# Loads cast by the DMA on one queue, and q and k in 72-partition runs, in a fused sliding-window attention and FFN kernel

## The chip, the cores and the metric

The kernel runs on one NeuronCore of a Trainium2 chip. The metric is device time in microseconds (us) of one execution, median over runs. The engines are TensorE (PE; its weight loads are PEld), VectorE (DVE), ScalarE (ACT), GpSimd (POOL) and SyncE (SP), which here only issues DMAs. 16 DMA engines serve all queues.

## The reference

Attention over q, k, v of shape (8 batches, 8 heads, 576 positions, 64), then an FFN over the 4608 tokens. Heads 0 to 3 see a window of the last 32 positions ("plain"), heads 4 to 7 every fourth of the last 128 ("dilated").

```python
rel = pos[:, None] - pos[None, :]
mask_plain = (rel >= 0) & (rel < 32)
mask_dil = (rel >= 0) & (rel < 128) & (rel % 4 == 0)
attn = softmax(where(mask, q @ k.T / 8, -1e9))      # per batch and head, f32
x = (attn @ v).transpose(0, 2, 1, 3).reshape(4608, 512)
h = relu(x @ w_in)                                  # w_in 512 x 2048
out = (h * h) @ w_out                               # w_out 2048 x 512
```

## The kernel before

**Attention** works on one batch and on pairs of heads: pair e (0 to 3) is heads 2e and 2e+1, pairs 0 and 1 plain, 2 and 3 dilated. `qT` holds q transposed, with the two heads' 64 dimensions one above the other on the partitions (rows 0 to 63 and 64 to 127) and positions along the free side; for dilated pairs the positions are sorted by residue modulo 4, so that a dilated window becomes a band again. `kbd` and `vbd` (two of the latter, for batches in turn) hold k and v as nine blocks of 64 positions, block-diagonal over the two heads: one head's block in rows and columns 0 to 63, the other's in 64 to 127, zeros elsewhere, written once by memsets. So one matmul over 128 rows serves both heads.

For each pair: `t_main` transposes q, then k, on PE against an identity into a PSUM tile `pa`, and copies evacuate it to `qT` and `kbd` (plain pairs on ACT, L209 and L223; dilated pairs on DVE, L204 and L218). `scores` (two halves) does the banded matmuls into `pa`, an Exp on ACT (L261) and a mask multiply on DVE (L262). `pv` (two halves) does P times V into `po` and, against a matrix `ones`, the row sums into `pd` (L304), then the reciprocal as Ln and Exp on ACT (L306, L307) and the product on DVE into `xT` (L310, L317), which the FFN reads. PSUM has four buffers for the FFN (`pf`), two for `pa`, one for `po` and one for `pd`.

**Loads.** SP's queue brings q, k and v as f32 into `raw` tiles, one set for all batches. Of q and k the first 512 positions are loaded with four consecutive positions on a partition (1 KB runs, L112) and the last 64 apart (`load_rem`, L120, 256 B runs); v by L131, L135 and L139. POOL then casts everything to bf16: `cast_qk` (L157, L163) into `rb` tiles, `cast_v` (L173) into the blocks of `vbd`. `t_rem` transposes the last 64 positions of all four pairs together and evacuates them with four DVE copies (L183, L186, L192). The FFN weights come on POOL's queue, cast by the DMA (L375, L380).

**FFN** takes 512 tokens at a time (9 tiles). A tile has 32 groups of four matmuls 128x512: 16 of `g1` (L343, then ReLU on ACT, L347, and a square on DVE, L348) and 16 of `g2` (L354; every fourth ends with a copy on ACT, L360, and a store by SP, L361).

**The order is written out by hand** (manual schedule; each engine executes in program order). Batch 0 is loaded, cast and its whole attention done before the first FFN group. Then, in the loop over tiles t, the loads of batch t+2 are issued first, and the attention of batch t+1 is woven between the groups: `attention_steps` gives each step the number of the group after which it is put (pair e begins at 1 + 7e: q, then k one later, scores at +3 and +4, pv at +6 and +8). The casts of batch t+2 are put on POOL four groups before the tile's end; POOL has nothing else, and starts each as soon as its data and its target are free.

Of the kernel before, what the change touches and what calls it, by code (L numbers as in the profile page):

```python
# [16 lines left out]
def _masks() -> np.ndarray:  # L17

    j = np.arange(64)[:, None]
    c = np.arange(96)[None, :]
    band = ((c - j >= 0) & (c - j < WIN)).astype(np.float32)
    kr, km = j % RES, j // RES
    cc = np.arange(64)[None, :]
    qr, qm = cc // 16, cc % 16
    rem = ((kr == qr) & (qm - km >= 0)).astype(np.float32)
    one = np.concatenate([band, rem], axis=1)
    return np.concatenate([one, one], axis=0).astype(ml_dtypes.bfloat16)  # L30
# [3 lines left out]
def kernel(  # L34
# [23 lines left out]
    MAIN = 512  # L58
# [8 lines left out]
    raw_pool = ctx.enter_context(tc.tile_pool(name="raw", bufs=1))  # L67
# [15 lines left out]
    ident = const.tile([P, P], bf16, name="ident")  # L83
    ones = const.tile([P, P], bf16, name="ones")
    mk = const.tile([P, 160], bf16, name="mk")
# [12 lines left out]
    raws = {}  # L98

    def load_qk(b: int, es):  # L100
        if b not in raws:
            raws[b] = {
                "q": raw_pool.tile([P, H, RES * D], f32, name="qraw"),
                "k": raw_pool.tile([P, H, RES * D], f32, name="kraw"),
                "qr": raw_pool.tile([64, H, D], f32, name="qrem"),
                "kr": raw_pool.tile([64, H, D], f32, name="krem"),
                "v": raw_pool.tile([P, NE, NB, D], f32, name="vraw"),
            }
        r = raws[b]
        hs = slice(2 * es[0], 2 * es[-1] + 2)  # L110
        for nm, src in (("q", q), ("k", k)):
            nc.sync.dma_start(  # L112
                r[nm][:, hs, :],
                src[b, hs, 0:MAIN, :].rearrange("h (p j) d -> p h (j d)", j=RES),
            )

    def load_rem(b: int):
        r = raws[b]
        for nm, src in (("qr", q), ("kr", k)):
            nc.sync.dma_start(  # L120
                r[nm][:, :, :], src[b, :, MAIN:S, :].rearrange("h p d -> p h d")
            )

    def load_v(b: int):
        r = raws[b]["v"]
        for hl in range(2):
            rows = slice(64 * hl, 64 * hl + 64)
            for e in range(NE):
                h = 2 * e + hl
                if e < NE // 2:  # L130
                    nc.sync.dma_start(  # L131
                        r[rows, e, :, :], v[b, h].rearrange("(i p) d -> p i d", p=64)
                    )
                else:
                    nc.sync.dma_start(  # L135
                        r[rows, e, 0:8, :].rearrange("p (m r) d -> p m (r d)", r=RES),
                        v[b, h, 0:MAIN, :].rearrange("(m p r) d -> p m (r d)", p=64, r=RES),
                    )
            nc.sync.dma_start(  # L139
                r[rows, NE // 2 : NE, 8, :],  # L140
                v[b, H // 2 + hl : H : 2, MAIN:S, :].rearrange("h p d -> p h d"),
            )


    rbs = {}

    def cast_qk(b: int, eng=None):
        eng = eng or nc.gpsimd
        r = raws[b]
        rbs[b] = {  # L150
            "q": rb_pool.tile([P, NE, RES, P], bf16, name="qb"),
            "k": rb_pool.tile([P, NE, RES, P], bf16, name="kb"),
            "qr": rb_pool.tile([64, NE, P], bf16, name="qrb"),
            "kr": rb_pool.tile([64, NE, P], bf16, name="krb"),
        }
        for nm in ("qr", "kr"):
            eng.tensor_copy(  # L157
                rbs[b][nm][:, :, :].rearrange("p e c -> p (e c)"),
                r[nm][:, :, :].rearrange("p h d -> p (h d)"),
            )  # L160
        for e in range(NE):
            for nm in ("q", "k"):
                eng.tensor_copy(  # L163
                    rbs[b][nm][:, e, :, :].rearrange("p j (h d) -> p h j d", h=2),
                    r[nm][:, 2 * e : 2 * e + 2, :].rearrange("p h (j d) -> p h j d", j=RES),
                )

    def cast_v(b: int):
        r = raws[b]["v"]
        for e in range(NE):  # L170
            for hl in range(2):
                rows = slice(64 * hl, 64 * hl + 64)
                nc.gpsimd.tensor_copy(vbd[b % 2][rows, e, :, 64 * hl : 64 * hl + 64], r[rows, e, :, :])  # L173


    def t_rem(b: int):
        ps = ps_a.tile([P, 1024], bf16, name="pa")
        for n, nm in enumerate(("qr", "kr")):
            for e in range(NE):
                c0 = 256 * n + 64 * e  # L180
                nc.tensor.transpose(ps[:, c0 : c0 + 64], rbs[b][nm][:, e, :], ident[0:64, 0:64])
        half = NE // 2
        nc.vector.tensor_copy(  # L183
            qT[:, 0:half, MAIN:S], ps[:, 0:128].rearrange("p (e c) -> p e c", c=64)
        )
        nc.vector.tensor_copy(  # L186
            qT[:, half:NE, :].rearrange("p e (r m) -> p e r m", r=RES)[:, :, :, 128:M],
            ps[:, 128:256].rearrange("p (e m r) -> p e r m", e=half, r=RES),
        )
        for hl in range(2):  # L190
            rows = slice(64 * hl, 64 * hl + 64)
            nc.vector.tensor_copy(  # L192
                kbd[rows, :, 8, 64 * hl : 64 * hl + 64],
                ps[rows, 256:512].rearrange("p (e c) -> p e c", c=64),
            )

    def t_main(b: int, e: int, nm: str):
        ps = ps_a.tile([P, 1024], bf16, name="pa")
        for j in range(RES):
            nc.tensor.transpose(ps[:, P * j : P * j + P], rbs[b][nm][:, e, j, :], ident[:, :])  # L200
        dil = e >= NE // 2
        if nm == "q":
            if dil:
                nc.vector.tensor_copy(  # L204
                    qT[:, e, :].rearrange("p (r m) -> p r m", r=RES)[:, :, 0:128],
                    ps[:, 0:MAIN].rearrange("p (r m) -> p r m", r=RES),
                )
            else:
                nc.scalar.copy(  # L209
                    qT[:, e, 0:MAIN].rearrange("p (m r) -> p m r", r=RES),  # L210
                    ps[:, 0:MAIN].rearrange("p (r m) -> p m r", r=RES),
                )
            return
        for hl in range(2):
            rows = slice(64 * hl, 64 * hl + 64)
            cols = slice(64 * hl, 64 * hl + 64)
            if dil:
                nc.vector.tensor_copy(  # L218
                    kbd[rows, e, 0:8, cols].rearrange("p (m r) c -> p r m c", r=RES),
# [183 lines left out]
    for _, step in attention_steps(0):  # L403
        step()
# [51 lines left out]
```

## Time and profile before

| What | us |
|---|---|
| median of 3 runs (399.03 to 404.46) | 400.42 |
| the profiled execution | 401.11 |
| its span in the profile | 399.3 |
| PE busy (modelled ends) | 321.9 |
| ACT, DVE, POOL busy | 208.5, 179.8, 98.3 |
| first FFN matmul begins | 62.1 |
| chain that ended last: PE 57%, ACT 13%, issue 10%, DVE 9% | |

The span is what the profile shows between the first and the last instruction; 1.8 us of the profiled execution lie outside it. Times within the trace count from the span's start. A group row gives line, engine, operation, target and source tile, shapes, count, then busy us and mean ns of one, then the idle time ahead of it and what ended it. "x4" in a timeline row means four merged instructions.

### The profile page before, as it was taken

To read this page: it belongs to the slowest core of one execution; us is meant where nothing else is said; L and a number is where in the kernel's file an instruction comes from. 1 tells how busy PE (TensorE), PEld (TensorE's weight loads), DVE (VectorE), ACT (ScalarE), POOL (GpSimd) and SP (SyncE) were. 2 spreads that over 40 slices of the span, in tenths; PEclk is the share of its full clock that TensorE was granted. 3 is DMA by queue.
4 is the path that set the end of the run, shared out by engine and by line. 5 is a ranking of instruction groups with operands and counts; after the bars stand their busy time and mean duration, and the time that the engine had idled before them with its cause. 6 is when DMAs were issued, how large, how long until landed. Compare 5 with 4: busy or idle time off the path is not lost.

```text
span 399.3 us, 5896 instructions
## 1 busy us (share of the span) xinstructions
PE 321.9 (81%) x2199; PEld 169.1 (42%) x2240; DVE 179.8 (45%) x365; ACT 208.5 (52%) x421; POOL 98.3 (25%) x158
## 2 busy tenths in 40 slices
PE   0201447999979997899699986999699999999996
PEld 0101333555535553455345543555345555444442
DVE  7100346653475347635763468336833543420410
ACT  1201434954873487448734792469346954742631
POOL 6423578300073007400640046003700000000000
PEclk9999999999998999999969998999899999999999
DMA  8999998001790179018901690149111001001002
GB/s 189 228 209 242 238 262 123 3 26 54 240 144 26 54 239 144 29 53 249 134 0 54 209 198 2 54 157 236 17 54 54 0 29 53 28 10 70 28 26 80
DMA packets 60557, 42.37 MB, mean 106 GB/s; under 512 B 31344, under 2 KB 55920, under 8 KB 60528
## 3 DMA queue, kind: packets, MB, share of 16 engines
q1 hardware_dynamic: 56160, 37.76, 39.0%
q0 software_dynamic: 4224, 4.19, 6.2%
q8 instruction: 17, 0.28, 0.3%
q10 hardware_dynamic: 144, 0.04, 0.1%
q14 instruction: 12, 0.10, 0.1%
HBM read 36.74 MB, written 9.44 MB: 116 GB/s over the span
## 4 chain that ended last, share of the span: by engine, by line
PE 57%; ACT 13%; issue 10%; DVE 9%; SPq 5%; DMA 5%; POOL 0%; ACTq 0%; POOLq 0%
PE pf L354 25%; PE pf L343 22%; ACT rec L307 4%; ACT rec L306 4%; DMA vraw<-in_v_dram 4%; DVE kbd L218 3%; DVE h2T L348 3%; PE po L304 3%; PE pd L304 2%; ACT kbd L223 2%; SPq L131 2%; ACT h2T L347 2%; PE pa L200 2%; DVE pt L262 2%; SPq L135 1%
## 5 line engine op out<-in xcount | busy, mean ns | idle before, releaser
L343 PE MATMUL pf<-xT,w_in_sb 128*128 128x512 bf16 x559 | 139.4, 386 | 1.2 <-issue 0.2
L354 PE MATMUL pf<-w_out_sb,h2T 128*128 128x512 bf16 x552 | 137.1, 386 | 1.3
L348 DVE TENSOR_TENSOR h2T<-h2T 128x512 bf16<-128x512 bf16 x144 | 92.8, 651 | 68.5 <-ACT h2T L347 67.0
L347 ACT ACTIVATE h2T<-pf 128x512 bf16<-128x512 f32 x144 | 84.6, 597 | 23.8 <-PE pf L343 23.3
L343 PEld LDWEIGHTS <-w_in_sb 128*128 128x128 bf16 x576 | 52.6, 99 | 51.7 <-issue 1.9
L354 PEld LDWEIGHTS <-h2T 128*128 128x128 bf16 x576 | 52.6, 99 | 51.1 <-issue 2.2
L306 ACT ACTIVATE rec<-pd 128x320 f32<-128x320 f32 (+1 forms) x64 | 26.3, 410 | 77.7 <-PE pd L304 77.7
L304 PE MATMUL po<-pt,vbd 128*128 128x96 bf16 (+3 forms) x320 | 24.2, 211 | 43.3 <-DVE pt L262 19.5
L173 POOL CAST vbd<-vraw 64x576 bf16<-64x576 f32 x64 | 46.4, 725 | 14.6 <-DMA vraw<-in_v_dram 11.3
L261 ACT ACTIVATE pt<-pa 128x480 bf16<-128x480 f32 (+1 forms) x64 | 32.3, 512 | 32.3 <-PE pa L246 27.4
L304 PEld LDWEIGHTS <-vbd 128*128 128x128 bf16 x320 | 22.1, 105 | 59.9 <-issue 30.1
L157 POOL CAST qrb<-qrem 64x512 bf16<-64x512 f32 x8 | 4.9, 606 | 164.3 <-PE pf L343 58.2
L310 DVE TENSOR_TENSOR xT<-po,rec 128x288 bf16<-128x288 f32 x32 | 14.7, 458 | 56.7 <-ACT rec L307 56.7
L360 ACT COPY osb<-pf 128x512 f32<-128x512 f32 x36 | 21.1, 587 | 35.7 <-PE pf L354 34.7
L317 DVE TENSOR_TENSOR xT<-po,rec 128x320 bf16<-128x320 f32 (+1 forms) x32 | 14.6, 456 | 37.3 <-ACT rec L307 33.9
L307 ACT ACTIVATE rec<-rec 128x320 f32<-128x320 f32 (+1 forms) x64 | 28.3, 443 | 2.0
L262 DVE TENSOR_TENSOR pt<-pt,mask_d 128x416 bf16<-128x416 bf16 (+1 forms) x32 | 12.8, 402 | 27.0 <-ACT pt L261 27.0
L304 PE MATMUL pd<-pt,ones 128*128 128x160 bf16 (+5 forms) x160 | 23.7, 250 | 0.0
L163 POOL CAST kb<-kraw 128x512 bf16<-128x512 f32 x32 | 19.4, 607 | 3.7 <-DMA kraw<-in_k_dram 3.7
L163 POOL CAST qb<-qraw 128x512 bf16<-128x512 f32 x32 | 19.4, 607 | 1.4 <-DMA qraw<-in_q_dram 1.4
L262 DVE TENSOR_TENSOR pt<-pt,mask_p 128x480 bf16<-128x480 bf16 (+1 forms) x32 | 16.9, 531 | 5.4 <-ACT pt L261 5.1
L223 ACT COPY kbd<-pa 64x512 bf16<-64x512 bf16 x32 | 18.3, 573 | 1.5 <-PE pa L200 1.3
(44 smaller groups left out, 183.0 us busy)
## 6 DMA issues: line engine op xcount, KB each, us to landing
out_dram<-osb SPq DMA_DIRECT2D x36, 256.0 KB, 2.0
qraw<-in_q_dram SPq DMA_DIRECT2D x7, 1024.0 KB, 5.7
kraw<-in_k_dram SPq DMA_DIRECT2D x7, 1024.0 KB, 8.5
vraw<-in_v_dram SPq DMA_DIRECT2D x32, 144.0 KB, 5.9
vraw<-in_v_dram SPq DMA_DIRECT2D x32, 128.0 KB, 5.4
w_in_sb<-in_moe_w_in_dram POOLq DMA_DIRECT2D x4, 512.0 KB, 13.1
w_out_sb<-in_moe_w_out_dram POOLq DMA_DIRECT2D x4, 512.0 KB, 25.2
qraw<-in_q_dram SPq DMA_DIRECT2D x2, 512.0 KB, 9.8
```

Source lines behind the costliest of these rows:

```text
L163: eng.tensor_copy(rbs[b][nm][:, e, :, :].rearrange("p j (h d) -> p h j d", h=2), r[nm][:, 2 * e : 2 * e + 2, :].rearrange("p h (j d) -> p ...
L173: nc.gpsimd.tensor_copy(vbd[b % 2][rows, e, :, 64 * hl : 64 * hl + 64], r[rows, e, :, :])
L223: nc.scalar.copy(kbd[rows, e, 0:8, cols].rearrange("p i (m r) -> p i m r", r=RES), ps[rows, 0:MAIN].rearrange("p (r i m) -> p i m r", r=RE ...
L261: nc.scalar.activation(pt[:, off : off + n], ps[:, 0:n], ACT.Exp, scale=SCALE)
L262: nc.vector.tensor_tensor(out=pt[:, off : off + n], in0=pt[:, off : off + n], in1=mask, op=ALU.mult)
L304: nc.tensor.matmul(oo, lh, rh, start=(x == 0), stop=(x == len(g) - 1), skip_group_check=True)
L306: nc.scalar.activation(rec[:, 0:n], d[:, 0:n], ACT.Ln)
L307: nc.scalar.activation(rec[:, 0:n], rec[:, 0:n], ACT.Exp, scale=-1.0)
L343: nc.tensor.matmul(ps1[:, :], w_in_sb[:, kt, P * f : P * f + P], xT[:, kt, tk0 : tk0 + NT], start=(kt == 0), stop=(kt == KT - 1),)
L347: nc.scalar.activation(h2[:, f, :], ps1[:, :], ACT.Relu)
L348: nc.vector.tensor_tensor(out=h2[:, f, :], in0=h2[:, f, :], in1=h2[:, f, :], op=ALU.mult)
L354: nc.tensor.matmul(cur[m][:, :], h2[:, f, P * m : P * m + P], w_out_sb[:, f, :], start=(f == 0), stop=(f == NF - 1),)
```

## The change

- q, k and v are loaded by POOL's queue, which casts them to bf16 on the way: q and k into `rb` tiles, v straight into the blocks of `vbd`. The `raw` tiles, `load_rem`, `cast_qk`, `cast_v` and `t_rem` are gone.
- q and k of a head lie on 72 partitions with 8 consecutive positions each (plain: 2 KB runs), or, for dilated heads, as two halves of 4 positions each (1 KB runs).
- `t_main` transposes per head, four transposes of a 72x128 block (two positions of 64 dimensions) into 72 columns each. The result has even positions (of the pair in the block) on rows 0 to 63 and odd ones on rows 64 to 127, so each evacuation copy takes one head and one half of the rows and moves it to that head's rows: dilated q is a DVE copy of 288 elements, dilated k DVE copies of 256 and 32, plain q and k an ACT copy of 288 each.
- The identity and the ones matrix come with the masks from DRAM; the memsets are put in another order.
- The loads of batch 0 are issued pair by pair in the order 0, 2, 1, 3, then the weights (w_in in two parts, not four), then batch 1. The last 64 positions of v of both dilated pairs come with the last pair's load.
- The attention of batch 0 (`first_attention`) is pipelined over the pairs and uses the `pf` buffers for its transposes. In FFN tile 0 the steps of batch 1 begin at group 12 with 5 groups a pair; later tiles begin at 0 with 7 a pair. The pairs go in the order 0, 2, 1, 3.

The diff, cut to its core:

```diff
     def load_qk(b: int, es):
...
+                if es_[0] < NE // 2:
+                    nc.gpsimd.dma_start(
+                        rbs[b][nm][:, hs, :], src[b, hs, :, :].rearrange("h (p j) d -> p h (j d)", j=JT)
+                    )
+                else:
+                    nc.gpsimd.dma_start(
+                        rbs[b][nm][:, hs, :].rearrange("p h (a x) -> p (h a) x", a=2),
+                        src[b, hs, :, :].rearrange("h (a p r) d -> p (h a) (r d)", a=2, r=RES),
+                    )
+    def load_v(b: int, es):
+        dst = vbd[b % 2]
...
+                if e < NE // 2:
+                    nc.gpsimd.dma_start(
+                        dst[rows, e, :, rows], v[b, h].rearrange("(i p) d -> p i d", p=64)
+                    )
+                    continue
+                for m in range(2):
+                    nc.gpsimd.dma_start(
+                        dst[rows, e, RES * m : RES * m + RES, rows],
+                        v[b, h, 256 * m : 256 * m + 256, :].rearrange("(p r) d -> p r d", r=RES),
+                    )
+        if es[-1] == NE - 1:
+            for hl in range(2):
+                rows = slice(64 * hl, 64 * hl + 64)
+                nc.gpsimd.dma_start(
+                    dst[rows, NE // 2 : NE, 8, rows],
+                    v[b, H // 2 + hl : H : 2, 512:S, :].rearrange("h p d -> p h d"),
+                )
+    def t_main(b: int, e: int, nm: str, pool=None, name="pa"):
+        ps = (pool or ps_a).tile([P, 1024], bf16, name=name)
...
+        for hl in range(2):
+            for jp in range(JT // 2):
+                pos = 2 * (jp % 2) + jp // 2 if dil else jp
+                nc.tensor.transpose(
+                    pv_[:, hl, PT * pos : PT * pos + PT], rbs[b][nm][:, 2 * e + hl, P * jp : P * jp + P], ident[0:PT, 0:PT]
+                )
         for hl in range(2):
             rows = slice(64 * hl, 64 * hl + 64)
+            for jj in range(2):
+                src = pv_[64 * jj : 64 * jj + 64, hl, :]
...
+    def first_attention(b: int):
+        o = ORDER
+        for x in range(NE + 2):
+            for nm, half in (("q", 0), ("k", 1)):
+                if x < NE:
+                    t_main(b, o[x], nm, ps_f, "pf")
+                if 1 <= x <= NE:
+                    scores(b, o[x - 1], half)
+                if x >= 2:
+                    pv(b, o[x - 2], half)
...
+    for e in ORDER:
+        load_qk(0, [e])
+        load_v(0, [e])
...
     load_qk(1, [0, 1, 2, 3])
+    load_v(1, [0, 1, 2, 3])
+    first_attention(0)
     for t in range(NTILES):
         groups = ffn_groups(t)
+        steps = attention_steps(t + 1, 12 if t == 0 else 0, 5 if t == 0 else 7) if t + 1 < B else []
```

More of the change, by code (lines that the diff above doesn't have):

```diff
@@ L8 @@
 from concourse import mybir
-from concourse.masks import make_identity
 from concourse._compat import with_exitstack
@@ L57 @@
     NB = S // 64
-    MAIN = 512
+    PT = 72
+    JT = S // PT
     NT = 512
@@ L95 @@
     mk_dram = nc.inline_tensor(_masks(), name="mask_patterns")
-    raws = {}
+    rbs = {}
     def load_qk(b: int, es):
[L101 to L107, printed above, removed]
-            }
[L109 to L115, printed above, removed]
@@ L139, in load_v @@
[L139 to L166, printed above, removed]
@@ L168, in cast_v @@
[L168 to L219, printed above, removed]
-                    ps[rows, 0:MAIN].rearrange("p (r m c) -> p r m c", r=RES, m=2),
-                )
-            else:
-                nc.scalar.copy(
-                    kbd[rows, e, 0:8, cols].rearrange("p i (m r) -> p i m r", r=RES),
-                    ps[rows, 0:MAIN].rearrange("p (r i m) -> p i m r", r=RES, i=8),
-                )
@@ L383 @@
         )
-    make_identity(nc, ident[:])
-    nc.vector.memset(kbd[0:64, :, :, 64:128], 0.0)
-    nc.vector.memset(kbd[64:128, :, :, 0:64], 0.0)
-    nc.vector.memset(ones[:, :], 0.0)
-    nc.vector.memset(ones[0:64, 0:64], 1.0)
-    nc.vector.memset(ones[64:128, 64:128], 1.0)
-    for i in range(2):
-        nc.vector.memset(vbd[i][0:64, :, :, 64:128], 0.0)
-        nc.vector.memset(vbd[i][64:128, :, :, 0:64], 0.0)
     nc.vector.tensor_copy(
```

105 lines of the change are left out of this document (59 added, 46 removed).

## The prediction

> **What bounds the kernel now.** I read the page's head first, then the busy time by stretch, cut where an FFN token tile begins (the columns are length, then PE, PEld, DVE, ACT, POOL busy with counts, TensorE clock, DMA share, GB/s).
>
> ```profile
> core 0: us, PE busy (x) PEld busy (x) DVE busy (x) ACT busy (x) POOL busy (x), PEclk, DMA share, GB/s
> 0.00:62.10 62.10, 14.56 (x136) 11.37 (x138) 17.74 (x38) 14.29 (x30) 29.53 (x51) 1.00 1.12 226
> 62.10:100.89 38.79, 36.31 (x259) 18.86 (x264) 20.46 (x42) 24.41 (x51) 10.89 (x17) 1.00 0.20 44
> 100.89:140.81 39.92, 36.36 (x260) 19.19 (x264) 21.52 (x42) 24.28 (x51) 11.58 (x18) 0.96 0.48 116
> ...
> 263.71:304.70 40.99, 36.35 (x260) 19.14 (x264) 22.50 (x42) 24.27 (x51) 11.58 (x18) 0.96 0.48 113
> 304.70:340.31 35.61, 34.55 (x260) 18.43 (x264) 16.25 (x42) 24.07 (x51) 0.00 (x0) 1.00 0.08 31
> 340.31:368.04 27.73, 27.62 (x127) 12.49 (x128) 7.26 (x17) 11.93 (x21) 0.00 (x0) 1.00 0.10 39
> 368.04:399.30 31.26, 27.47 (x125) 12.35 (x126) 6.80 (x16) 12.48 (x21) 0.00 (x0) 1.00 0.11 43
> ```
>
> Two things stand out. For 62.1 us TensorE does 14.6 us of work while the DMA engines are full (share 1.12). Then it is the bound, but the five tiles from 100.89 to 304.70 take 40.8 us each where the seventh, which has the same attention work and no POOL casts, takes 35.61. What the casts cost is seen in the timeline of one such tile, with the seventh tile's own group last:
>
> ```profile
> 114.57 4.20 DVE L348 TENSOR_TENSOR h2T<-h2T 128x512 bf16<-128x512 bf16 x2 [1.26 <-ACT h2T L347]
> 117.64 6.37 POOL L173 CAST vbd<-vraw 64x576 bf16<-64x576 f32 x8
> 119.61 0.36 PE L304 MATMUL po<-pt,vbd 128*128 128x96 bf16 x5 [2.50 <-DVE pt L262]
> ...
> L348 DVE TENSOR_TENSOR h2T<-h2T 128x512 bf16<-128x512 bf16 x16 | 6.8, 425 | 6.5 <-ACT h2T L347 6.2
> ```
>
> Two squares that need 0.425 us each take 4.20 beside the casts, and PE idles 2.50 us. The start is a chain of loads, casts and first attention: the wait for `vraw` from the chain that ended last, then the POOL cast it released and the PV steps by their first matmul.
>
> ```profile
> 21.87 14.45 DMA vraw<-in_v_dram
> ...
> 36.45 5.00 POOL L173 CAST vbd<-vraw 64x576 bf16<-64x576 f32 x7 [9.26 <-DMA vraw<-in_v_dram]
> 51.98 0.48 PE L304 MATMUL po<-pt,vbd 128*128 128x96 bf16 x5 [1.64 <-DVE pt L262]
> 54.24 0.48 PE L304 MATMUL po<-pt,vbd 128*128 128x96 bf16 x5 [1.04 <-DVE xT L310]
> 61.09 0.48 PE L304 MATMUL po<-pt,vbd 128*128 128x96 bf16 x5 [1.47 <-DVE xT L310]
> ```
>
> **Part 1, the loads.** All of them move to POOL's queue. A batch is now 576 packets of 2 KB (q, k of the plain heads), 1152 of 1 KB (dilated heads) and 4608 of 256 B, written as 128 B (v, in every head, since its destination runs are 64 bf16). The packet times before, from the DMA rows of three windows (10 to 20, 104 to 108 and 111 to 116 us), then POOL's issues, a DVE memset beside them, and the time a store takes to land:
>
> ```profile
> q0 software_dynamic: 1352, 1.35, 79.4%
> DMA packets 1364, 1.38 MB, mean 345 GB/s; under 512 B 16, under 2 KB 1364, under 8 KB 1364
> DMA packets 2673, 0.91 MB, mean 182 GB/s; under 512 B 2364, under 2 KB 2672, under 8 KB 2672
> ...
> 1.24 3.12 POOL L375 DMA_DIRECT2D w_in_sb<-in_moe_w_in_dram  x4 [0.80 <-POOLq L440]
> 4.31 3.01 POOL L380 DMA_DIRECT2D w_out_sb<-in_moe_w_out_dram  x4
> 4.15 1.02 DVE L391 MEMSET vbd<- 64x1152 uint32 x1 [0.28 <-issue]
> ...
> out_dram<-osb SPq DMA_DIRECT2D x36, 256.0 KB, 2.0
> ```
>
> A cast 2 KB packet occupies its engine 0.794 x 16 x 10 us / 1352 = 94 ns; a plain 1 KB one 16 x 4 / 1364 = 47 ns, the same per byte; a plain 256 B one 16 x 5 / 2673 = 30 ns. A cast 256 B packet is not in the trace: its bounds are 30 ns (no dearer than plain) and 94 ns (the software queue's only row, however small the packet); a gain below 30 is excluded because nothing gets fewer bytes to read. I take 40, nearer the row with the same bytes. Then a batch needs T = (576 x 94 + 1152 x 47 + 4608 x 40) / 16 = 3.4 + 3.4 + 11.5 = 18.3 us (15.4 to 34). POOL's issue, 0.78 us a DMA, is 22 x 0.78 = 17 us for the first batch and 18 x 0.78 = 14 for each later one: under T, so hidden by the transfers. The weights are 4096 x 94 / 16 = 24.0 us, and they now stand between batch 0 and batch 1. With 2 us to land (the last row): batch 0 at 1.2 + 18.3 + 2 = 21.5, the first half of w_in at 27.6, batch 1 at 1.2 + 18.3 + 24 + 18.3 + 2 = 63.8. From batch 2 on a load has a tile of some 41 us to hide in; beyond T = 41 it would no longer. A v load waits on POOL for the PV of two batches earlier; behind it stand loads only. SP keeps just the stores. The Trainium skill ("DMA: Bandwidth & Descriptors", the section on why a DMA increments its semaphore by 16) gives the largest divisor up to 16 of the slowest dimension as the number of engines, which would be 12 for 72 partitions; by it q and k would be an estimated 9 us and not 6.8, and the whole some 4 us longer. No run here shows it.
>
> **Part 2, the first attention.** It is now pipelined over the pairs (order 0, 2, 1, 3), but the remainder of v for both dilated pairs is loaded last, and PE's in-order queue holds PV of pair 2 for it, with the transposes of pair 3's k and the scores of pair 1 behind. From 21.5 six PV halves follow, each held by the one PSUM tile `po`; their spacing is 54.24 - 51.98 = 2.26, for the plain pair some 2.5: 6 x 2.4 = 14.4, and 1 for pair 3's copies on DVE among them. FFN tile 0 starts at 37 instead of 62.1. At an undisturbed 27.73 / 32 = 0.865 us a group, PE reaches PV of pair 2 of batch 1 (group 23) after 24 groups (20.8), 3.7 us of attention (pair 0, pair 2 short of its PV, pair 1's transposes: nearly half of the 35.61 - 27.73 us that a tile has beside its groups) and 2.3 of waits priced below, at 63.7: as batch 1 lands. Then 8 groups (6.9), the rest of the attention (3.3), two more waits (3.0) and two PV halves that hang behind the last group (4.6) follow: tile 1 starts at 63.8 + 17.8 = 81.6, against 100.89. In general, where loads bind, that is 45 + 2T. The identity and the ones now come with the masks on ACT's queue, and the six memsets of 1.02 us stand in another order; they cost nothing, as batch 0's last piece at 21.5 sets this path, and at most 1 us if it came sooner.
>
> **Part 3, a tile with attention.** Gone are the casts: base 35.6. PE's transposes become 64 of 72 columns for 32 of 128 and 8 of 64. The evacuations become twice as many or more, since each copy moves one head and one position half: for a plain pair 8 ACT copies of 64x288 for 1 of 128x512 and 2 of 64x512; for a dilated one, on DVE, 4 of 288, 4 of 256 and 4 of 32 for 1 and 2 of 512, and the four remainder copies (L183 to L192) go.
>
> ```profile
> L223 ACT COPY kbd<-pa 64x512 bf16<-64x512 bf16 x32 | 18.3, 573 | 1.5 <-PE pa L200 1.3
> L306 ACT ACTIVATE rec<-pd 128x288 f32<-128x288 f32 x32 | 13.2, 413 | 27.3 <-PE pd L304 27.3
> L306 ACT ACTIVATE rec<-pd 128x256 f32<-128x256 f32 x16 | 6.1, 381 | 14.5 <-PE pd L304 14.5
> L218 DVE COPY kbd<-pa 64x512 bf16<-64x512 bf16 x32 | 13.3, 417 | 0.2
> L192 DVE COPY kbd<-pa 64x256 bf16<-64x256 bf16 x16 | 4.5, 283 | 0.1
> L183 DVE COPY qT<-pa 128x128 bf16<-128x128 bf16 x8 | 1.7, 218 | 5.3 <-PE pa L181 5.3
> ```
>
> An ACT copy of 288 is about 0.40 us (0.413 for the reciprocal's form; 0.573 less 224 elements at 0.83 ns is 0.39): 1.6 for q and 1.6 for k of a plain pair, where 0.58 and 1.16 stood. On DVE 256 costs 0.283 and 512 0.417, so 0.52 ns an element: 288 is 0.30, 32 by the line through 128 and 256 is 0.17; q 1.2, k 4 x (0.283 + 0.17) = 1.8 where 0.84 stood. All this is off PE, but the scores wait for it, and every FFN group waits behind the scores. The rows that time this are the first attention steps of the seventh tile, the pieces of the chain that ended last for transposes, and a dilated pair behind a PV:
>
> ```profile
> 304.54 1.13 PE L343 MATMUL pf<-xT,w_in_sb 128*128 128x512 bf16 x4
> 305.71 0.60 ACT L347 ACTIVATE h2T<-pf 128x512 bf16<-128x512 f32 x1 [0.38 <-PE pf L343]
> 308.59 1.16 ACT L223 COPY kbd<-pa 64x512 bf16<-64x512 bf16 x2
> 309.85 0.33 PE L255 MATMUL pa<-qT,kbd 128*128 128x96 bf16 x4
> ...
> 101.86 0.34 PE pa L181 x8
> 103.17 0.22 PE pa L200 x4
> ...
> 83.68 0.34 PE L304 MATMUL po<-pt,vbd 128*128 128x32 bf16 x5
> 84.65 0.42 ACT L307 ACTIVATE rec<-rec 128x256 f32<-128x256 f32 x1
> 85.44 0.84 DVE L218 COPY kbd<-pa 64x512 bf16<-64x512 bf16 x2
> 86.34 0.22 PE L240 MATMUL pa<-qT,kbd 128*128 128x96 bf16 x1 [0.20 <-DVE kbd L218]
> ```
>
> Transposes: 64 x 0.34 / 8 = 2.7 against 8 x 0.22 + 0.34 = 2.1, so +0.6. Pair 0: ACT does ReLU, q, ReLU, k from 305.71: 0.5 + 1.6 + 0.55 + 1.6 ends at 309.96; PE, from 305.60, has transposes 0.34, a group 0.87, transposes 0.34 and two groups 1.73, and is at the scores at 308.88: it waits 1.1, where today it waits nothing (copies end 309.75, scores 309.85). Pairs 2 and 3: the PV in front starts at 83.68 and DVE reaches the copies at 85.44, behind that PV's product; PE could be at the scores at 83.68 + 0.35 + 0.22 + 1.73 = 85.98, and waits 0.36. With copies 0.97 longer and transposes 0.12 longer it waits 1.2, twice. Pair 1: its k copies stand on ACT behind the q copies, a ReLU and pair 2's Ln and Exp (84.65 + 0.42 is 1.4 after its PV): they end 4.2 after that PV starts, PE is there after 2.4, waits 1.8. Sum 5.3, against 0.36 twice and next to nothing for the plain pairs now: +4.6. Bounds: 0, if the engines' idle time absorbs it, and 8, if each of the four waits also drags the exponent behind it. I take the sum in order. Tile: 35.6 + 0.6 + 4.6 = 40.8, say 41. So what the casts gave back the copies take.
>
> **Sum.** 45 + 2 x 18.3 = 81.6; six tiles 1 to 6 at 41 = 246; tiles 7 and 8 unchanged, 27.7 + 31.3 = 59: span 386.6. The profiled execution took 401.11 for a span of 399.3, 1.8 outside: 388.4. Its 401.1 stands 0.2% over the median 400.42, which leaves 388.
>
> **Rivals.**
> *The copies stay hidden.* ACT is busy 24.07 of 35.61 us and gets 3 more, DVE 16.25 and 2.4 more: neither is full, which speaks for it. The in-order chain above and 0.36 us of wait today speak against. Tiles of 37: 388 - 24 = 364.
> *The small cast packets are slow.* One mechanism, in the start: v's 256 B packets take the software queue's 94 ns. T = 34, tile 1 starts at 45 + 68 = 113, the total, 351 + 2T, is 419: slower than before. It decides from T = 25 us, 63 ns a packet. For it: 94 is the only software-queue row, and small packets already run at 182 GB/s against 345. Against it: casting cost nothing per byte. The Trainium skill (same page, Specifications) puts line rate at 512 B and a read-modify-write below; the trace agrees in direction, 30 ns for 256 B against 47 for 1 KB, and no run shows it for a cast.
> *POOL's issues hold DVE as its casts do.* 14 us of issues in a tile for 11.58 of casts: +5 in seven tiles, 388 + 35 = 423. Against it, memsets keep 1.02 us beside POOL's issues (rows above). The Trainium skill ("SBUF — State Buffer", Who interferes with whom) says that DVE with two SBUF inputs collides with GpSimd's reads, and infers that generating descriptors needs writes: by it nothing is held here. Its summary's advice, to issue a DMA that lies beside DVE work from a hardware queue, speaks against the change all the same.
>
> **How the numbers follow.** The forecast 0.59, hidden copies 0.13, slow packets 0.20, held DVE 0.08. The forecast's own range is 376 to 400 (tiles 39 to 43, T 15 to 22). About 2% is what a measurement can tell, that is 392 and 408. Faster: hidden copies 0.13 and 0.42 of the forecast, 0.55. Same: its other 0.17 and 0.08 of the slow packets (T up to 28), 0.25. Slower: the rest, 0.20. The range, 364 to 419, reaches to the middle of the two nearer rivals and leaves out some 0.2.
>
> **What would show it.** Right: FFN's first matmul near 37 us and tile 1 near 82; no long L348; before the first scores of each pair PE idles 1 to 2 us and names the copies; tiles near 41. Wrong: tiles of 37, or no such idle; packets of the software queue well over 60 ns in v's stretch; PE waiting on `vbd` or `qb` loads beyond tile 0; L348 near 0.9 us while POOL issues.

## The result, and the profile after

| Kernel | median us | runs | span of the profiled execution |
|---|---|---|---|
| before, same chip | 400.49 | 4 (399.03 to 404.46) | 399.3 |
| after | 385.92 | 4 (385.62 to 386.30) | 383.9 |

The ratio is 0.962 (95% interval 0.955 to 0.969): faster by 3.8%. The forecast was 388.0. The page's head of the kernel after:

```profile
span 383.9 us, 6344 instructions
PE 319.0 (83%) x2389; PEld 168.4 (44%) x2432; DVE 164.0 (43%) x474; ACT 243.2 (63%) x501; POOL 104.5 (27%) x158
```

Now the busy time by stretch, cut where an FFN tile begins, in the columns that the prediction shows for before:

```profile
core 0: us, PE busy (x) PEld busy (x) DVE busy (x) ACT busy (x) POOL busy (x), PEclk, DMA share, GB/s
0.00:32.20 32.20, 14.62 (x160) 11.66 (x162) 18.76 (x49) 18.34 (x40) 22.70 (x36) 1.00 1.11 144
32.20:77.50 45.30, 38.37 (x285) 19.68 (x290) 19.35 (x57) 29.97 (x62) 27.86 (x41) 1.00 1.25 144
77.50:118.60 41.10, 36.14 (x281) 19.12 (x286) 18.87 (x57) 27.94 (x59) 12.73 (x19) 0.96 0.63 76
118.62:159.77 41.15, 34.94 (x284) 18.62 (x288) 18.68 (x56) 28.52 (x60) 12.11 (x18) 1.00 0.58 71
...
283.20:324.00 40.80, 34.65 (x284) 18.44 (x287) 18.63 (x56) 28.52 (x60) 0.00 (x0) 1.00 0.07 27
324.00:352.00 28.00, 27.84 (x128) 12.70 (x130) 6.85 (x17) 11.89 (x20) 0.00 (x0) 1.00 0.10 38
352.00:383.90 31.90, 27.52 (x126) 12.35 (x126) 6.80 (x16) 12.42 (x21) 0.00 (x0) 1.00 0.11 42
```

The start fell from 62.1 to 32.2 us. Nothing else became shorter to speak of: tile 0 went from 38.79 to 45.30, the tiles with casts from 40.8 to 41.1, and the seventh, which never had casts, from 35.61 to 40.80. So 29.9 us were won at the start and half of that was given back. In a tile of 41.15 us PE is busy 34.94; before, in the seventh tile, it was busy 34.55 of 35.61. The timeline of the tile from 118.62 shows what it waits for (the score matmuls of pairs 0, 2, 1 and 3 at which PE waited, in order of time, and ACT ahead of pair 0):

```profile
120.02 1.93 ACT L182 COPY qT<-pa 64x288 bf16<-64x288 bf16 x4
121.97 0.60 ACT L325 ACTIVATE h2T<-pf 128x512 bf16<-128x512 f32 x1
122.46 1.90 ACT L187 COPY kbd<-pa 64x288 bf16<-64x288 bf16 x4
...
124.42 0.39 PE L219 MATMUL pa<-qT,kbd 128*128 128x96 bf16 x5 [1.82 <-ACT kbd L187]
133.18 0.22 PE L204 MATMUL pa<-qT,kbd 128*128 128x96 bf16 x1 [0.91 <-DVE kbd L173]
133.62 0.22 PE L204 MATMUL pa<-qT,kbd 128*128 128x96 bf16 x1 [0.19 <-DVE kbd L173]
143.71 0.39 PE L219 MATMUL pa<-qT,kbd 128*128 128x96 bf16 x5 [2.30 <-ACT kbd L187]
152.03 0.22 PE L204 MATMUL pa<-qT,kbd 128*128 128x96 bf16 x1 [0.47 <-DVE kbd L173]
152.48 0.22 PE L204 MATMUL pa<-qT,kbd 128*128 128x96 bf16 x1 [0.20 <-DVE kbd L173]
```

Every wait of PE names the evacuation copies, and together they are 1.82 + 1.10 + 2.30 + 0.67 = 5.9 us of the tile. None of the three engines is full (ACT is busy 28.5 us of 41, DVE 18.7, PE 34.9), so the suspect is the place of the copies in the order and not their work; runs 1, 2 and 8 test it. The groups of the copies, and the FFN's square beside them (mean ns in the last but one field):

```profile
L182 ACT COPY qT<-pa 64x288 bf16<-64x288 bf16 x56 | 26.6, 474 | 1.2 <-PE pa L159 0.7
L187 ACT COPY kbd<-pa 64x288 bf16<-64x288 bf16 x56 | 26.2, 467 | 0.5
...
L326 DVE TENSOR_TENSOR h2T<-h2T 128x512 bf16<-128x512 bf16 x144 | 60.7, 425 | 101.4 <-ACT h2T L325 99.9
L169 DVE COPY qT<-pa 64x288 bf16<-64x288 bf16 x56 | 17.0, 303 | 1.1 <-PE pa L159 0.6
L173 DVE COPY kbd<-pa 64x256 bf16<-64x256 bf16 x56 | 16.0, 286 | 0.6
L177 DVE COPY kbd<-pa 64x32 bf16<-64x32 bf16 x56 | 12.3, 219 | 0.0
```

L326, the square that took 2.1 us beside POOL's casts, has a mean of 0.425 over all its 144 instructions, the price that it had in the seventh tile of the kernel before. At the start, the timeline shows POOL's last issue for batch 0, two PV halves and FFN's first matmul; the last row is POOL's last v issue for batch 1:

```profile
15.03 1.24 POOL L143 DMA_DIRECT2D vbd<-in_v_dram  x2
...
19.48 0.50 PE L268 MATMUL po<-pt,vbd 128*128 128x96 bf16 x5 [1.08 <-DVE xT L281]
...
31.22 0.48 PE L268 MATMUL po<-pt,vbd 128*128 128x96 bf16 x5 [1.47 <-DVE xT L274]
32.23 1.06 PE L321 MATMUL pf<-xT,w_in_sb 128*128 128x512 bf16 x2 [0.22 <-issue]
33.48 12.36 PE L321 MATMUL pf<-xT,w_in_sb 128*128 128x512 bf16 x48 [0.18 <-DVE xT L274]
...
51.86 1.24 POOL L143 DMA_DIRECT2D vbd<-in_v_dram  x2
```

And the packets of a stretch from 84 to 90 us in which only v was under way, with the time from issue to landing:

```profile
q0 software_dynamic: 2000, 0.24, 63.6%
...
vbd<-in_v_dram POOLq DMA_DIRECT2D x2, 16.0 KB, 2.1
```

A small cast packet takes 0.636 x 16 x 6 us / 2000 = 30.5 ns.

### The profile page after: what moved, and what is told of

The parts are those of the page before. It is cut to its first block, busy times and chain, and to the rows that moved or that the text cites. A ratio compares the mean times of both kernels' runs of the same rounds, so it can differ in the third digit from the quotient of the medians.

```text
span 383.9 us, 6344 instructions
## 1 busy us (share of the span) xinstructions
PE 319.0 (83%) x2389; PEld 168.4 (44%) x2432; DVE 164.0 (43%) x474; ACT 243.2 (63%) x501; POOL 104.5 (27%) x158
## 2 busy tenths in 40 slices
DMA packets 66190, 28.33 MB, mean 74 GB/s; under 512 B 44528, under 2 KB 60528, under 8 KB 66160
## 4 chain that ended last, share of the span: by engine, by line
PE 53%; ACT 26%; DVE 12%; issue 5%; POOL 2%; DMA 1%; ACTq 0%; POOLq 0%
PE pf L332 25%; PE pf L321 20%; ACT kbd L187 7%; ACT qT L182 7%; ACT rec L271 4%; ACT h2T L325 4%; ACT rec L270 4%; DVE kbd L173 3%; DVE xT L281 3%; DVE qT L169 2%; PE pa L219 2%; DVE kbd L177 2%; PE po L268 2%; PE pd L268 2%; DVE h2T L326 1%
## 5 line engine op out<-in xcount | busy, mean ns | idle before, releaser
L332 PE MATMUL pf<-w_out_sb,h2T 128*128 128x512 bf16 x553 | 133.0, 379 | 1.3
L326 DVE TENSOR_TENSOR h2T<-h2T 128x512 bf16<-128x512 bf16 x144 | 60.7, 425 | 101.4 <-ACT h2T L325 99.9
L136 POOL DMA_DIRECT2D vbd<-in_v_dram x64 | 39.1, 615 | 35.3 <-DMA qb<-in_q_dram 16.6
L338 ACT COPY osb<-pf 128x512 f32<-128x512 f32 x36 | 21.1, 585 | 41.1 <-PE pf L332 41.1
L219 PE MATMUL pa<-qT,kbd 128*128 128x96 bf16 x144 | 12.0, 214 | 26.0 <-ACT kbd L187 25.9
L115 POOL DMA_DIRECT2D qb<-in_q_dram x9 | 7.0, 775 | 89.5 <-PE pa L159 88.7
L274 DVE TENSOR_TENSOR xT<-po,rec 128x288 bf16<-128x288 f32 x32 | 14.6, 458 | 38.8 <-ACT rec L271 38.8
L182 ACT COPY qT<-pa 64x288 bf16<-64x288 bf16 x56 | 26.6, 474 | 1.2 <-PE pa L159 0.7
L187 ACT COPY kbd<-pa 64x288 bf16<-64x288 bf16 x56 | 26.2, 467 | 0.5
L131 POOL DMA_DIRECT2D vbd<-in_v_dram x32 | 24.1, 773 | 8.4 <-DMA w_out_sb<-in_moe_w_out_dram 8.4
L219 PEld LDWEIGHTS <-kbd 128*128 128x128 bf16 x144 | 8.8, 102 | 36.1 <-ACT kbd L187 32.8
L268 PE MATMUL pd<-pt,mk 128*128 128x32 bf16 (+5 forms) x160 | 22.8, 243 | 0.0
```

Source lines behind the costliest of these rows:

```text
L136: nc.gpsimd.dma_start(dst[rows, e, RES * m : RES * m + RES, rows], v[b, h, 256 * m : 256 * m + 256, :].rearrange("(p r) d -> p r d", r=RES),)
L182: nc.scalar.copy(qT[rows, e, :].rearrange("p (u a j) -> p j u a", a=JT // 2, j=2)[:, jj, :, :], src.rearrange("p (a u) -> p u a", a=JT // 2),)
L187: nc.scalar.copy(kbd[rows, e, :, rows].rearrange("p i (u a j) -> p j i u a", a=JT // 2, j=2)[:, jj, :, :, :], src.rearrange("p (a i u) -> ...
L219: nc.tensor.matmul(ps[:, n : n + w], kbd[:, e, i, :], qT[:, e, 64 * i : 64 * i + w], start=True, stop=True)
L268: nc.tensor.matmul(oo, lh, rh, start=(x == 0), stop=(x == len(g) - 1), skip_group_check=True)
L326: nc.vector.tensor_tensor(out=h2[:, f, :], in0=h2[:, f, :], in1=h2[:, f, :], op=ALU.mult)
```

## The experiments

The theory after the result: the start gained by the order of the loads; in the tiles the gain of the casts is real, but the copies, which the scores in PE's order wait for, take it back. The rivals: the tiles are held by something else (POOL's many DMA issues, contention, the added transposes), or they were never held by the casts. Where one run is given, it stands beside seven runs of the kernel before on the same chip, whose medians were 399.3 to 400.1.

**1. Half the copies** (one run). `qT` and `kbd` are zeroed once and the odd position half is not evacuated; PE's work stays.

```diff
-            for jj in range(2):
+            for jj in range(1):
```

> The changed kernel with half of its evacuation copies: the copies of the odd positions (rows 64 to 127 of the transposes) are left out, so odd positions of q and k stay zero; qT and kbd are zeroed whole at the start instead. My theory: a tile with attention takes 41.15 us because the scores wait 5.9 us for the copies (1.8 pair 0, 1.1 pair 2, 2.3 pair 1, 0.7 pair 3); with half of them (ACT 1.9 us less per plain pair, DVE 0.9 to 1.0 less per dilated k) about 0.5 us of wait is left, so tiles of 36 us and 385.9 - 7 x 5.2 = 350 us, at most 1 us worse for the memsets at the start. Rival: the tile's excess over 35.6 us is the work of POOL's issues and the loads beside it; then tiles stay at 41 and the time at 384 to 387.

342.57 us. The busy time of one of its tiles:

```profile
113.75:148.93 35.18, 34.66 (x289) 18.47 (x288) 15.74 (x45) 24.65 (x53) 12.15 (x18) 1.00 0.63 81
```

All of PE's work, transposes too, fits in 35.2 us, with POOL's 18 issues in the tile. The added transposes and POOL are not what holds it. The time is 7 us under the expectation: the tiles are 35.2 and not 36, and the start is shorter too (FFN's first matmul at 30.4, not 32.2). This run says that the copies cost the time, but not whether by their work or by their place.

**2. The same work, scores later** (4 runs). Only the group numbers in `attention_steps` change, so that the scores of a pair, and with them its PV steps (except those of pair 3), come one or two FFN groups later; no instruction is added or removed.

```diff
-            steps.append((s + 3, lambda e=e: scores(b, e, 0)))
-            steps.append((s + 4, lambda e=e: scores(b, e, 1)))
-            steps.append((s + 6, lambda e=e: pv(b, e, 0)))
-            steps.append((s + 8, lambda e=e: pv(b, e, 1)))
+            d = (3, 4, 6, 8) if pace == 5 else ((5, 6, 8, 10), (4, 5, 7, 9), (5, 6, 8, 10), (4, 5, 6, 8))[x]
+            steps.append((s + d[0], lambda e=e: scores(b, e, 0)))
+            ...
```

> The changed kernel with the same instructions, but in tiles 1 to 6 the scores and PV of a plain pair stand two FFN groups later (one for the dilated pairs), so that each copy has 1.7 us (0.87) more before the scores need it. My theory (PE waits for the copies, in order): of 5.9 us of wait per tile about 0.5 to 1 is left, tiles of 36 to 36.5 and 385.9 - 6 x 4.9 = 356 us (353 to 360). Rival A: ScalarE is at its limit in the first half of a tile (ReLU and 16 copies), so moving the scores only moves the wait to the FFN groups: 380 to 386. Rival B: the excess is POOL's: 386.

353.52 us (353.23 to 354.80), 0.887 (0.884 to 0.889) of before. A tile, and the largest wait for a copy that is left in it:

```profile
112.26:148.25 35.99, 35.10 (x289) 18.79 (x288) 18.47 (x56) 28.33 (x60) 12.13 (x18) 1.00 0.63 81
```

```profile
134.94 0.39 PE L219 MATMUL pa<-qT,kbd 128*128 128x96 bf16 x5 [0.18 <-ACT kbd L187]
```

ACT's and DVE's busy time are those of the changed kernel (28.33 and 28.52, 18.47 and 18.68); the tile is 5.1 us shorter and the waits of 5.9 are gone. So it is the place. This is the run that settles the main point: with the same work on ACT and DVE the copies cost next to nothing, once the scores stand one or two groups further behind them.

**3. Before, without the casts of the later batches** (one run). The kernel before, with batches 2 to 7 attending on the cast data of batches 0 and 1.

```diff
-                cast_qk(t + 2)
-                cast_v(t + 2)
+                rbs[t + 2] = rbs[t % 2]
```

> The kernel before, with POOL's casts left out from batch 2 on (the loads are still done; the attention of later batches reads the cast data of batches 0 and 1). My theory: the casts cost 5.15 us in each of the tiles 1 to 5 and 3.2 in tile 0, so 400.5 - 29 = 371 us and tiles of 35.6. Rival: those tiles are long because of the transfers that go on in them, which stay: 400 us.

374.87 us. The tiles that took 40.8 now begin every 35.60 us (135.51, 171.11, 206.71); a stretch of that length:

```profile
125.67:161.27 35.60, 34.81 (x266) 18.45 (x264) 16.25 (x43) 24.06 (x50) 0.00 (x0) 1.00 0.56 131
```

So the casts did cost 5.2 us a tile in tiles 1 to 5. Tile 0 stayed as it was (38.3 us, before 38.8), where the expectation had 3.2 less; most of the 4 us by which it missed lie there. In the changed kernel the tiles are at 41 all the same: what came in its place is what run 2 removes.

**4. The first attention not pipelined** (one run). Batch 0's attention in the order of the kernel before.

```diff
-    first_attention(0)
+    for _, step in attention_steps(0, 0, 7):
+        step()
```

> The changed kernel with the attention of batch 0 done pair after pair in the order of the tiles' step list (transposes in the pa buffers), not pipelined. My theory: the start is set by the chain of eight PV halves, and a serial pair takes some 7 us (44.12 to 51.98 and 51.98 to 58.83 in the kernel before), so FFN begins near 39 to 40 us instead of 32.2, and the time is 385.9 + 7 = 393 us. Rival: the start is set by the loads (batch 0 lands near 18 us, weights behind it) and the order of the pairs costs nothing: FFN at 32 to 33 and 386 us.

391.87 us. FFN's first matmul:

```profile
37.30 1.44 PE L321 MATMUL pf<-xT,w_in_sb 128*128 128x512 bf16 x3
```

37.3 for 32.2 (39 to 40 was expected): of the 29.9 us won at the start, the pipelining, with the `pf` buffers that it uses, is 5.1.

**5 and 6. v loaded twice** (one run each). Every v block is loaded a second time into a tile that nobody reads: in run 5 for batches 2 to 7, in run 6 for all. This doubles v's issues on POOL and its packets.

```diff
+        load_v_to(vbd[b % 2], b, es)
+        if b >= 2:              # run 6: b >= 0
+            load_v_to(vdum, b, es)
```

> The changed kernel that loads v of batches 2 to 7 a second time, into a spare tile that nothing reads. It doubles the 4608 small cast packets of a batch, POOL's issues for them (14 more DMAs, some 9 us), and the traffic. My theory: from tile 1 on the loads hide (POOL is through with a batch 17 to 19 us into a tile of 41), so 385 to 387 us. Rivals: POOL's issues hold DVE, or the loads already bind: +1 us or more in each of five tiles, 391 us and up.

> The same for all batches. In batch 0 the second v of three pairs stands ahead of the last pair's remainder (8 of 14 DMAs, 5.5 us of POOL's issues), so PV of pair 2 starts near 24 us, not 19.5, and FFN at 37. Batch 1 lands 9 us later, near 64, when PE gets to the PV that needs it, so nothing more is added: 391 us (389 to 395). If, as my forecast had it, the loads bind tile 0 as well (a start of 45 + 2T), both batches' delay counts: 9 + 9 us, 403 us.

Run 5 took 385.07 us, like the changed kernel. A stretch of a tile's length:

```profile
160.00:201.00 41.00, 34.86 (x284) 18.57 (x288) 18.68 (x56) 28.38 (x61) 21.05 (x32) 1.00 0.80 84
```

POOL is busy 21.05 us for 12.1, DVE is still busy 18.68 for the same 56 instructions, and the tile still takes some 41 us. From batch 2 on the loads are hidden with room to spare, and POOL's issues do not hold DVE. The rule of the Trainium skill that the prediction named ("SBUF — State Buffer", Who interferes with whom: a DVE instruction with two SBUF inputs collides with GpSimd's reads, and generating descriptors is inferred to need writes) agrees with this run.

Run 6 took 393.37 us, 7.5 more than the changed kernel and 2.4 more than expected. FFN starts at 36.8, as expected, but PE then waits for q of batch 1:

```profile
52.11 0.43 PE L165 MATMUL pa<-mk,qb 72*128 72x72 bf16 x8 [2.69 <-DMA qb<-in_q_dram]
```

The second v of a batch is 4608 x 30.5 / 16 ns = 8.8 us of packets. Of the 17.6 us added in the first two batches 7.5 show, so little slack is left there: the loads come near to binding, though in the changed kernel itself they do not. The 403 us of loads that bind tile 0 did not come.

**7. The plain pairs' k copies moved from ACT to DVE** (one run).

```diff
-                    nc.scalar.copy(
+                    nc.vector.tensor_copy(          # at L187
```

> The changed kernel with the k copies of the plain pairs on VectorE and not on ScalarE; everything else, the number of copies too, as it is. My theory: pair 0 waits because ReLU, q, ReLU and k stand one behind the other on ScalarE, and pair 1 because pair 2's reciprocal stands between them besides; with k beside q the waits fall from 1.8 and 2.3 to some 0.5 each, tiles of 38, 385.9 - 6.5 x 3.0 = 366 us (362 to 371), if a copy that writes every other element costs DVE 0.3 to 0.45 us. Rival: the number of copies counts, wherever they run, and DVE (18.7 of 41 us busy) delays its squares instead: 380 to 388.

406.95 us: a miss by 41, and longer than the kernel before (399.94 on that chip). The timeline of a tile, around pair 0's scores, and the busy time of the next:

```profile
125.10 1.94 ACT L182 COPY qT<-pa 64x288 bf16<-64x288 bf16 x4
127.06 1.57 ACT L325 ACTIVATE h2T<-pf 128x512 bf16<-128x512 f32 x3
127.69 0.42 DVE L326 TENSOR_TENSOR h2T<-h2T 128x512 bf16<-128x512 bf16 x1 [2.03 <-ACT h2T L325]
128.03 1.93 DVE L187 COPY kbd<-pa 64x288 bf16<-64x288 bf16 x4
130.02 0.39 PE L219 MATMUL pa<-qT,kbd 128*128 128x96 bf16 x5 [2.33 <-DVE kbd L187]
130.24 1.72 PE L321 MATMUL pf<-xT,w_in_sb 128*128 128x512 bf16 x4
...
168.92:212.77 43.85, 36.67 (x285) 19.12 (x288) 22.19 (x64) 25.14 (x52) 12.50 (x19) 0.96 0.60 65
```

DVE is free from 125.66, but in DVE's order the square L326 stands ahead of the copies, and that square waits 2.03 us for a ReLU which stands on ACT behind the four q copies. So the k copies wait for the q copies after all, by way of the FFN. The wait is longer than before the edit (2.33 for 1.82), and the four matmuls after it take 1.72 us where the same four take 1.03 in the changed kernel. The tiles are 43.9 to 45.3. Of the 2.7 us by which the one from 168.92 is longer than the changed kernel's, 1.0 is longer waits before the plain pairs and 1.7 is PE itself (36.67 busy for 34.94), at a granted clock of 0.96. A copy of plain k costs DVE 0.47 us, just over the 0.45 that the expectation allowed; but what failed is that it had counted the work on each engine and not the chain in front of it.

**8. The plain pairs' q copies moved instead** (one run). The same edit at L182, with k left on ACT; q stands ahead of the square.

> The changed kernel with the q copies of the plain pairs on VectorE, k left on ScalarE (the other way round from the run with k on VectorE, 407 us). My theory: there DVE's k copies stood behind the square of a ReLU that itself stood behind ScalarE's q copies, so the two engines still worked one after the other. With q on DVE nothing on ScalarE stands behind it: q can start one square after the first ReLU, k right after the second. Pair 0 then waits 0.5 and not 1.8, pair 1 0.9 and not 2.3, tiles of 38.4, 385.9 - 6.5 x 2.8 = 368 us (364 to 372). Rival: plain copies are simply dearer on DVE, because its squares come late (as the run with k seemed to say): 386 us or more.

368.14 us. A tile, and the waits before the plain pairs' scores in it:

```profile
115.57:154.04 38.47, 35.27 (x289) 18.62 (x288) 22.33 (x64) 24.95 (x53) 12.11 (x18) 1.00 0.65 75
...
118.93 0.39 PE L219 MATMUL pa<-qT,kbd 128*128 128x96 bf16 x5 [0.51 <-ACT kbd L187]
...
136.86 0.39 PE L219 MATMUL pa<-qT,kbd 128*128 128x96 bf16 x5 [0.94 <-ACT kbd L187]
```

1.82 became 0.51 and 2.30 became 0.94. With the chain counted, the number comes out. Runs 7 and 8 each put four copies of 64x288 a plain pair on DVE, at the same price (0.472 and 0.478 us), and are 39 us apart. They are not the same copies: in run 7 they stand in DVE's order behind a square that waits for ACT's q copies, in run 8 nothing on ACT stands ahead of them; and part of the 39 us is run 7's lower clock.

**9. Scores later, tile 0 included** (4 runs). Run 2, and in tile 0 the attention begins at group 10 with 4 groups between pairs, where the change has 12 and 5.

> The kernel with the scores later in tiles 1 to 6 (353.5 us), and in tile 0 the attention of batch 1 from group 10 on with 4 groups a pair, scores 4 after the q transposes, so that nothing hangs behind the last group. My theory: tile 0 takes 44 us there, of which some 1.8 + 1.5 are waits for copies and 3 to 4 the PV halves behind the last group; q and k of batch 1 land at 41 to 43 us, when group 10 ends: 349 us (347 to 352). Rival: v of batch 1 lands too late for an earlier start, and PE waits for it instead: 353 us.

352.50 us (351.46 to 353.00), 0.883 (0.881 to 0.884) of before. Against run 2's 353.5, on another chip, that is no gain that can be told, and 349 was expected. In tile 0 PE waits for no load, against the rival; new waits for ACT, its copies (0.82 and 1.50 us) and its exponents, took the place of the PV tail.

**10. Runs 8 and 9 together** (4 runs).

> The kernel with the scores later and tile 0 changed (352.5 us), and the plain q copies on VectorE. My theory: tiles 1 to 6 are at 36.0 there and PE's own work is 35.1, so little is left, 0.3 us a tile; tile 0 waits for ScalarE some 3 us, of which half goes: 349 us (347 to 351). Rival: DVE's copies now delay the dilated pairs': 352 to 356.

341.87 us (341.50 to 342.48), 0.855 (0.849 to 0.860) of before. A stretch in its steady part:

```profile
107.00:142.00 35.00, 34.92 (x292) 19.14 (x291) 22.58 (x65) 25.02 (x53) 12.72 (x19) 1.00 0.66 86
```

PE is busy 34.92 of 35.00 us, so next to no wait is left in this stretch for another order to remove. The time is 7 us under the expectation. That had taken the 35.1 us that PE was busy in run 2's tile for PE's own work and allowed a gain of 0.3 us a tile; the tiles went from 36.0 to 34.5, and six times the 1.2 us more is the 7. It is the shortest of the runs with all the work in, 11% under the changed kernel.

**11. The weights ahead of batch 0** (one run). The loads of batch 0 are put behind the DMAs of w_in and w_out, on the same queue.

```diff
-    for e in ORDER:
-        load_qk(0, [e])
-        load_v(0, [e])
 ...
+    for e in ORDER:
+        load_qk(0, [e])
+        load_v(0, [e])
```

> The changed kernel with the FFN weights issued ahead of batch 0 on POOL's queue. My theory: the queue is first in, first out, the weights take 24 us, and nothing of the start can begin without batch 0: FFN begins at 32 + 22 to 24 = 55 us, and the time is 385.9 + 22 = 408 us. So the order of need is most of what the start gains, and with the weights first the cast loads alone would leave the start near the 62 us of the kernel before. Rival: the queue's packets of both interleave over the 16 engines and batch 0 is only some 10 us later: 396 us.

406.04 us. FFN's first matmul:

```profile
51.76 1.44 PE L321 MATMUL pf<-xT,w_in_sb 128*128 128x512 bf16 x3
```

51.8 for 32.2: the wrong order costs 19.6 us. This is not a share of the 29.9 us won at the start, because in the kernel before the weights did not stand ahead of the loads but came beside them, on a queue of their own. Even with the weights first FFN begins 10.3 us sooner than before, where the expectation had some 7; what of this belongs to the casts that no longer stand between load and use was not measured apart. With the weights first the whole change would have gained nothing (406.04, and 400.05 for the kernel before on that chip).

## Why the prediction was right, step by step

The direction, the size and the mechanism of the tiles held: 388.0 said, 385.9 measured, and what the casts gave back the copies took. The account of the start and of tile 0 did not hold, and that the total is so near is partly luck: errors cancel.

**Batch 0 lands at 21.5, POOL's issues hidden under T: wrong.** A small cast packet takes 30.5 ns and not 40, close to the lower bound of the two. By this T is 3.4 + 3.4 + 4608 x 30.5 / 16 ns = 15.6 us. POOL issues batch 0 from 1.33 to 16.27, in 14.9 us (17 was said), and the last piece lands some 2 us after its issue, at about 18. Transfers and issues are so near each other that neither can be called the bound.

**Six PV halves follow the load: right in spacing, wrong in what starts them.** (31.22 - 19.48) / 5 = 2.35 us a half, said 2.4. But the first of the six, at 19.48, waits for the product of the half before it and not for the last v. In the chain that ended last, that product stands behind ACT, which works without a pause from 12.63 to 18.97: the four q copies of pair 1 (1.94 us), the four k copies (1.91), and between and behind them exponents and reciprocals. So the new copies set the start as well, in ACT's order; run 1, with half of them, begins FFN 1.8 us sooner. FFN starts at 32.2, said 37: the six halves begin 2.0 us before the landing that was forecast, and from there it takes 12.7 and not 15.4, because FFN's first matmul comes 1.0 us after the last half has begun, and not a whole spacing, and the 1 us for pair 3's copies is within the spacing.

**Tile 0 is bound by the loads (tile 1 at 45 + 2T): wrong.** POOL's last issue for batch 1 ends at 53.1 and lands at about 55, said 63.8, and PE waits for no load in tile 0. Two batches at T = 15.6 are 5.4 us of this; and the weights pass faster: from 20 to 30 us the queue wrote 2.05 MB, by which their 4.19 MB are an estimated 20.5 us and not 24.0. Tile 0 took 45.3, said 44.6, by other terms than mine: its first matmuls run slowly (48 in 12.36 us, where 12 x 0.865 is 10.4; they are 0.43 us apart until 36.8 and half of that behind it), and its waits name the copies and the PV tail. The 4.1 us by which tile 1 is early are the 4.8 of the start less 0.7 here.

**A tile of 41: right, with its parts off in both directions.** 5.9 us of waits, said 5.3; PE's transposes 0.5 less than said (eight take 0.28 us in the chain that ended last, so 64 take 2.2 and not 2.7). The ACT copy was the term mis-sized: 0.474 us, said 0.40, because I subtracted elements at the price of f32 forms; from the copy of 512 to that of 288 only 0.44 ns an element are saved, and not 0.83 (their access patterns differ too, so this is no price of an element). Two sets of four are 0.6 us longer, which is about what pair 0 (1.82, said 1.1) and pair 1 (2.30, said 1.8) wait beyond the forecast. DVE's 288 and 256 (0.303 and 0.286) were right; 32 took 0.219, said 0.17. Pair 2 waited 1.1, said 1.2, and pair 3 only 0.67, said 1.2; I did not trace why the two dilated pairs differ. The bound of 0 for these waits, "if the engines' idle time absorbs it", was not absurd: run 2 gets there with one or two groups more between copies and scores. That is what I should have seen and said, since a time of 353 lay in reach of the same work.

**The end: 59.9 us, said 59.** The last two tiles are 28.0 and 31.9, and for no reason that a run tells.

Sum of it: -4.1 at tile 1, +0.5 over six tiles, +0.9 at the end make 383.9 of the forecast span of 386.6.

**The rivals.** Hidden copies (364) fail by tiles of 41, and run 2 shows by how little. Slow cast packets (419) fail by 30.5 ns, against the 63 from which they would have decided. POOL's issues as a brake on DVE (423) fail by the tile from 283.20, which has no POOL work and takes 40.80, by L326 at 0.425 and by run 5.

## What to carry to other kernels

A cheaper load path can be paid for in evacuation copies, and what these cost depends less on their work than on where they stand: put the first reader far enough behind the copies in each engine's order (one or two FFN groups here, 32 us in all) before judging the layout. When work is moved to an idle engine, read the chain in front of it in that engine's order, not its busy time: four copies a pair, of the same size and price, were worth -18 us on DVE when nothing on ACT stood ahead of them (run 8), and +21 when a square that waited for ACT did (run 7; a lower clock is part of that). When all loads go through one queue, set the order of need first: the weights ahead of batch 0 cost 19.6 us here.

## What the runs showed of the hardware that was not expected

Waits of 2.33 to 2.82 us were followed by matmuls at a reduced clock. In run 7, the scores of the second plain pair, the matmuls behind them, and the granted clock of that stretch:

```profile
151.50 0.58 PE L219 MATMUL pa<-qT,kbd 128*128 128x96 bf16 x5 [2.82 <-DVE kbd L187]
151.88 1.91 PE L332 MATMUL pf<-w_out_sb,h2T 128*128 128x512 bf16 x4
```

```profile
148.00:156.00 8.00, 5.18 (x29) 2.37 (x27) 3.44 (x8) 2.70 (x6) 0.00 (x0) 0.79 0.00 0
```

Four matmuls take 1.91 us. Behind the wait of 2.30 us in the changed kernel (at 143.71, shown above) the same four keep their pace, while at the turn from tile 0 to tile 1 two shorter waits are followed by a slow stretch:

```profile
143.93 1.03 PE L332 MATMUL pf<-w_out_sb,h2T 128*128 128x512 bf16 x4
...
75.77 0.33 PE L268 MATMUL po<-pt,vbd 128*128 128x96 bf16 x5 [1.47 <-DVE xT L274]
...
77.74 0.58 PE L321 MATMUL pf<-xT,w_in_sb 128*128 128x512 bf16 x1 [0.81 <-DVE xT L274]
78.12 0.68 PE L159 MATMUL pa<-mk,qb 72*128 72x72 bf16 x8
78.61 1.90 PE L321 MATMUL pf<-xT,w_in_sb 128*128 128x512 bf16 x4
```

So the length of one wait does not decide alone; when it happens, four matmuls cost nearly a microsecond more. The clock records of the traces tell more. Up to the end of the program each reduced stretch is at half rate, lasts 3.41 us or twice that, and begins on a grid of 3.41 us (77.76 to 81.17 in the changed kernel). Over the 13 traces of this case, PE was idle (by the modelled ends of its matmuls) for 2.0 us or more in sum in 19 intervals of that grid that were themselves at full clock, and all 19 were followed by half rate; of 59 with 1.5 to 2.0 us idle, two were; with less, none. The waits of 1.47 and 0.81 us fall into one interval (74.34 to 77.76), the wait of 2.30 us spreads over two. This is read from the traces; no run varied it. The Trainium skill ("TensorE: Matmul & The Clock Gate", Part 1) puts the step down to half rate after an idle window of some 3.4 us; the traces agree on the window's length, but some 2 us idle within it were enough here, and the measurement decides: staying under that figure is not enough. The clock column does not show the start: the records of the changed kernel begin at 36.80, and the column has 1.00 for the time before, where the matmuls are 0.43 us apart.

A cast by the DMA cost nothing over a plain transfer for small packets (30.5 ns for 256 B read and 128 B written, against 30 for a plain 256 B packet before). POOL's issuing, 0.6 to 0.8 us a DMA, then takes about as long as the packets: 14.9 us beside some 15.6 for batch 0, so both have to be counted when such loads stand on the path.
